# Attention and a gated block on one core: the order of work planned with a clock per engine

## The chip, the cores and the metric

The kernel runs on 1 core of one Trainium2 chip. The metric is the device time of one execution in microseconds; lower is better. TensorE (PE in the profile) multiplies matrices into PSUM, ScalarE (ACT) does the exponentials, VectorE (DVE) and GpSimd (POOL) do elementwise work, SyncE (SP) issues the DMAs.

## The reference

One transformer block over 2048 rows of 640 columns, in bf16, with 32 heads of 20 columns:

```
def _A_ref(x, wqkv, wo):                                   # H = 32, Dh = 20
    qkv = (x @ wqkv).reshape(B, S, 3, H, Dh).transpose(2, 0, 3, 1, 4)
    q, k, v = qkv[0], qkv[1], qkv[2]
    scores = einsum("bhqd,bhkd->bhqk", q, k) * (Dh ** -0.5)
    o = einsum("bhqk,bhkd->bhqd", softmax(scores), v)
    return o.transpose(0, 2, 1, 3).reshape(B, S, D) @ wo
def _B_ref(x, w_gate, w_up, w_down):                       # F = 1728
    return ((x @ w_gate) * (x @ w_up)) @ w_down

h  = x + _A_ref(layernorm(x), A_wqkv, A_wo)
h2 = h + _B_ref(layernorm(h), B_w_gate, B_w_up, B_w_down)
```

The scores are 32 x 2048 x 2048 numbers, and each goes through an exponential.

## The kernel before

Heads are taken four at a time (a group; 8 groups `g`), each head on 32 partitions. The queries are cut into four blocks of 512 (`b`, a pass; the last block also in halves `A` and `B` for six of the groups), the keys into 16 tiles of 128 (`kt`). One **unit** is the scores of one head, one key tile and 512 queries: a matmul with 32 rows of weights (`L427`) into one PSUM bank. Three units in a row fill a **score tile** `sc` of three banks, of which there are two buffers; ScalarE makes one exponential over its 1536 columns into `E` (`L433`, six buffers). The **value matmuls** (`L597`) multiply `E` with the values and a column of ones; four heads sum side by side in one PSUM bank `acc`, over all keys of a group and a block (a **segment**). VectorE copies `acc` out (`L607`, `L612`); GpSimd multiplies by the reciprocals of the sums (`L529`).

Everything else that TensorE does is a **job**, a generator that stands in a queue: transposes of the first layer norm (`job_T`, `L252`), projections to queries and keys (`job_proj`, `L270`), values (`job_V`, `L284`), and, when all groups of a query block are done, that block's tail: the output projection (`out_mm`, `L812`), the second layer norm (`ln2_pieces` on VectorE, then transposes), the two gated sums (`glu_sum`, `L878`) and the last product (`job_y`, `L911`). All jobs share one PSUM bank `mi`, which VectorE empties before the next job may fill it. The layer norm pieces of VectorE stand in a second queue, `aux`; the first layer norm's square root is made on GpSimd in small steps, and VectorE's reciprocal (`L212`) waits for them.

VectorE also makes the exponentials of 80 units itself: for 20 segments, `emit_x` makes one unit per head with a score matmul of its own into `mi` (`L453`); `L463` scales it, and five passes follow (`L474` to `L477`, and `L468`): two masks that split an int32 into exponent and mantissa, and a polynomial of the mantissa.

The program is written out in a loop over the 656 score tiles, and each engine runs its instructions in the order in which the loop emits them. Per tile: the three score matmuls and the exponential; a job begun earlier goes on for up to `BUDGET` = 640 ns; up to four 512-column value matmuls of the tiles up to two back; `aux` pieces while an estimate of VectorE's load is below `AUX_LOAD`; passes of VectorE's units; and, if no job was going on, either a new unit of VectorE's or a new job for up to `START` = 440 ns:

```
        used = go_on(BUDGET) if i < n_tiles else BUDGET
        emit_AV(i if i >= n_tiles else i - 2 if i >= LAG else i - 4)
        while now["dve"] < AUX_LOAD and step_aux():
            pass
        if not used:
            if x_todo and cur["fresh"] and now["dve"] < X_LOAD and x_ready():
                emit_x()
            else:
                begin(START)
```

The estimate `now["dve"]` grows with each instruction given to VectorE and falls by `STEP` = 1331 ns with each tile. After the last tile, `last_tail` does the last 256 rows with all of TensorE; a second path, `general`, is in the program and is skipped unless the sums leave their range.

Of the kernel before, what the change touches and what calls it, by code (L numbers as in the profile page):

```python
# [12 lines left out]
I32 = mybir.dt.int32  # L13
ACT = mybir.ActivationFunctionType
# [32 lines left out]
SUM_HI = 1e15  # L47
NEXT = "next slot"
END = "end"
BUDGET = 640  # L50
START = 440
WARM = 58
LAG = 10
STEP = 1331
AUX_LOAD, X_LOAD = 1200, 900
SHIFT = 394.0
X_AHEAD, X_STEP, X_OUT = 8, 5, 6
LOG2E = 1.4426950408889634
X_SCALE = SM_SCALE * LOG2E * 2.0 ** 23
C3 = 0.07802454279127117  # L60
X_P, X_Q, X_R = -0.10261439735317812, 6.123365857342997, 5.794771205884579
EXP_BIAS = (SHIFT * SM_SCALE * LOG2E - 127.0) / LOG2E - math.log(C3) - SHIFT * SM_SCALE


@with_exitstack
def kernel(
# [153 lines left out]
    now = {"i": 0, "dve": 0}  # L220

    def dve(ns):

        now["dve"] += ns
# [71 lines left out]
    for ch in range(NB):  # L296
        for g in range(G1):
# [9 lines left out]
    X_KT = 2  # L307
    X_SEGS = [s for s, (p, g, _, _, kind) in enumerate(segs)
              if kind == "only" and p in "012"]

    tiles, cur_t, pos = [], [], 0
    for s, (p, g, lo, hi, _) in enumerate(segs):
        w = PASS[p][2]
        n = BANK // w
        for kt, j, k in [(kt, j, k) for kt in range(lo, hi, n) for j in range(HPG) for k in range(n)]:
            if s in X_SEGS and X_KT <= kt < X_KT + n:
                continue
            cur_t.append((s, kt + k, j, pos))
            pos += w
            if pos == EW:  # L320
                tiles.append((cur_t, EW))
                cur_t, pos = [], 0
# [3 lines left out]
    first_tile = {}  # L326
    for i, (us, _) in enumerate(tiles):
        for s, *_ in us:
            first_tile.setdefault(s, i)
    x_todo = deque((first_tile[s] - X_AHEAD + X_STEP * j, s, j) for s in X_SEGS for j in range(HPG))  # L330
    x_pieces = deque()
    x_made = {}
    x_put = []
    x_live = {"units": 0, "passes": 0}
# [6 lines left out]
    urgent = deque()  # L341
    aux = deque()
# [6 lines left out]

    def do(key, fn, front=False):  # L350
        def gen():
            fn()
            yield 0
        add(key, gen(), front)
# [9 lines left out]
    def step():  # L364
        if urgent and cur["fresh"]:
            if cur["gen"] is not None:
                jobs.appendleft((cur["key"], cur["gen"]))
            cur["key"], cur["gen"] = urgent.popleft()
# [4 lines left out]
        try:  # L373
            c = next(cur["gen"])
        except StopIteration:
            done.add(cur["key"])
            cur["gen"], c = None, END
        cur["fresh"] = c in (END, NEXT)
        return c
# [6 lines left out]
    def step_aux():  # L386
        while aux:
            try:
                dve(next(aux[0]) or 200)
# [3 lines left out]
        return False  # L393

# [5 lines left out]
    def go_on(ns):  # L400
        used = 0
        while not cur["fresh"] and used < ns:
            c = step()
            used += c if c not in (END, NEXT) else 0
        if not cur["fresh"]:
            return max(used, 1)
        return used

    def begin(ns):
        used = 0  # L410
        while used < ns:
            c = step()
            if c is None or c == NEXT or (c == END and used):
                break
            used += c if c != END else 0

    def emit_S(i):
# [6 lines left out]
        for s, kt, j, o in us:  # L424
# [6 lines left out]
                start=True, stop=True)  # L431
        e = ep.tile([P, EW], BF16, name="E")
        nc.scalar.activation(e[:, 0:n], sc[:, 0:n], ACT.Exp, bias=EXP_BIAS, scale=SM_SCALE)  # L433
        for s, kt, j, o in us:
            av_q.append((i, s, kt, j, e[:, o:o + PASS[segs[s][0]][2]]))

    def x_ready():
        due, s, _ = x_todo[0]
        p, g = segs[s][0:2]
        return (due <= now["i"] and x_live["units"] < X_OUT and x_live["passes"] < 2  # L440
                and ("q", PASS[p][0], g) in done and ("k", g, 0) in done)

    def emit_x():

        _, s, j = x_todo.popleft()
        p, g = segs[s][0:2]
        b, c0, w = PASS[p]
        n = BANK // w
        ensure(("k", g, X_KT // TPB))
        ensure(("q", b, g))  # L450
        ps = bank()
        for k in range(n):
            nc.tensor.matmul(  # L453
                ps[:, k * w:(k + 1) * w],
                lhsT=kT[g][SLOT * j:SLOT * (j + 1), (X_KT + k) * P:(X_KT + k + 1) * P],
                rhs=q_of(g, b, c0, w)[SLOT * j:SLOT * (j + 1), :],
                start=True, stop=True)
        v = xp.tile([P, BANK], I32, name="xv", bufs=2)
        m = xp.tile([P, BANK], F32, name="xm")
        t = xp.tile([P, BANK], F32, name="xt")  # L460
        e = xp.tile([P, BANK], BF16, name="xe", bufs=X_OUT)
        dve(690)
        nc.vector.tensor_scalar(v[:], ps[:], X_SCALE, 0.0, ALU.mult, ALU.max)  # L463
        x_live["units"] += 1
        x_live["passes"] += 1

        def last():
            nc.vector.scalar_tensor_tensor(e[:], t[:], X_R, v[:].bitcast(F32), ALU.add, ALU.mult)  # L468
            x_live["passes"] -= 1
            x_made.setdefault(s, []).append((j, e))  # L470
            if len(x_made[s]) == HPG:
                x_put.append([(now["i"], s, X_KT + k, j, e[:, k * w:(k + 1) * w]) for k in range(n) for j, e in x_made[s]])
        x_pieces.extend([
            (430, lambda: nc.vector.tensor_scalar(m[:].bitcast(I32), v[:], 0x007FFFFF, 0x3F800000, ALU.bitwise_and, ALU.bitwise_or)),  # L474
            (430, lambda: nc.vector.tensor_scalar(v[:], v[:], 0x7F800000, None, ALU.bitwise_and)),
            (690, lambda: nc.vector.scalar_tensor_tensor(t[:], m[:], X_P, m[:], ALU.add, ALU.mult)),  # L476
            (690, lambda: nc.vector.scalar_tensor_tensor(t[:], t[:], X_Q, m[:], ALU.add, ALU.mult)),  # L477
            (690, last)])

    def put_x():  # L480

        for units in x_put:
            s = units[0][1]
            at = next((k for k, u in enumerate(av_q) if u[1] > s), len(av_q))
            for u in reversed(units):
                av_q.insert(at, u)
        x_put.clear()

    def step_x(n):
        while n > 0 and x_pieces:  # L490
            ns, fn = x_pieces.popleft()
            dve(ns)
            fn()
            n -= 1

    def need_x(s):
        while len(x_made.get(s, ())) < HPG:
            if x_pieces:
                step_x(1)
                continue  # L500
            while not cur["fresh"]:
                step()
            emit_x()
# [64 lines left out]
    def emit_AV(upto):  # L568
# [9 lines left out]
        if acc["seg"] != s:  # L578
            if now["i"] < acc["from"]:
# [3 lines left out]
        most = 2 * QB * 2 // w  # L583
# [7 lines left out]
        for _ in range(ready):  # L591
            _, _, kt, j, e = av_q.popleft()
            if s in X_SEGS and kt == X_KT:
# [8 lines left out]
        acc["left"] -= ready  # L602
        if acc["left"] == 0:
# [9 lines left out]
            acc["seg"], acc["from"] = None, now["i"] + 2  # L613
# [81 lines left out]
    def gen_ln(ch):  # L695
        ts = range(ch * TPB, (ch + 1) * TPB)
        mv = small.tile([P, TPB, 2], F32, name="mv")
        while ch not in xs:
            yield STEP
# [89 lines left out]
    def new_st(rows_of):  # L789
# [3 lines left out]
        st["hh"] = [hp.tile([P, QB], BF16, name=f"hh{f}") for f in range(2 * FP)]  # L793
# [40 lines left out]
    def job_out(on, st, ts, key):  # L834
        pairs = [ts[k:k + 2] for k in range(0, len(ts), 2)]

        def T_pair(pair):
            for t in pair:
                while ("l2", key, t) not in done and end["pool"] is None and key is not None:
                    yield NEXT  # L840
# [48 lines left out]

    def job_glu(st, ts, order=tuple(range(FP))):  # L890
        c0, n = ts[0] * P, len(ts) * P
        hold = {}
        for k, fp in enumerate(order):
# [3 lines left out]
            for f2 in range(2):  # L897
                for m in range(2):
# [32 lines left out]
    def add_tail(b, ts):  # L931
# [16 lines left out]
        do(("load",) + key, ready)  # L948
# [255 lines left out]
```

## Time and profile before

| what | us |
|---|---|
| time, median of 3 runs (lowest, highest) | 978.65 (976.43, 979.57) |
| span of the profiled execution | 977.6 |
| ScalarE busy | 905.2 (93%) |
| of this, the 656 exponentials, L433 | 887.8 |
| TensorE busy in matmuls | 865.3 (89%) |
| VectorE busy | 576.8 (59%) |
| GpSimd busy | 64.6 (7%) |
| mean granted TensorE clock | 0.935 |

The span runs from the first instruction to the last of one profiled execution; the profiled execution has no device time of its own, and the median of the timed runs lies 1.05 us above its span. A group line of the profile names line, engine, operation, output and inputs with their shapes and the count, then the busy time, the mean of one instruction in ns, and the engine's idle time just before them with what ended it. In a timeline line the first two numbers are start and length in us. In a window line the columns are length, busy time of PE, PEld, DVE, ACT and POOL with counts, the granted clock, the DMA share and GB/s.

### The profile page before, as it was taken

How to read it: one execution, taken by the hardware profiler on the slowest of the kernel's cores; microseconds unless marked ns; L12 is line 12 of the kernel's file. 1: busy time of each engine (PE TensorE's matmuls, PEld its weight loads, DVE VectorE, ACT ScalarE, POOL GpSimd, SP SyncE). 2: the span in 40 equal slices, each digit the busy share in tenths (PEclk: the TensorE clock that was granted, in tenths of full speed). 3: DMA queues.
4: the chain of work that ended last, by engine and by line, in shares of the span. 5: the costliest groups of instructions: out<-in, count | busy, mean ns of one | idle time of the engine just before them, and what ended most of it. 6: DMA issues, size and time to landing. Idle time of an engine off the chain costs nothing.

```text
span 977.6 us, 17623 instructions
## 1 busy us (share of the span) xinstructions
PE 865.3 (89%) x6981; PEld 325.1 (33%) x7041; DVE 576.8 (59%) x1186; ACT 905.2 (93%) x692; POOL 64.6 (7%) x163
## 2 busy tenths in 40 slices
PE   6779998889989899999898988898889999989987
PEld 4223332222223222233232222233332333435455
DVE  7564367877777777777677677777143331143232
ACT  6689999999999899999999999999899999999941
POOL 4110001200000000000000000000000000000000
PEclk9999999999999599999778899999597999989989
DMA  6000000010014022101420222000602000211210
GB/s 182 4 24 1 1 25 24 13 32 27 5 47 146 12 66 59 40 13 33 180 67 12 66 67 60 12 22 23 163 1 66 14 13 20 67 36 40 81 35 17
DMA packets 67816, 44.42 MB, mean 45 GB/s; under 512 B 18504, under 2 KB 63404, under 8 KB 67728
## 3 DMA queue, kind: packets, MB, share of 16 engines
q1 hardware_dynamic: 67728, 43.23, 15.5%
q8 instruction: 57, 0.93, 0.4%
q14 instruction: 31, 0.25, 0.1%
HBM read 35.91 MB, written 7.30 MB: 44 GB/s over the span
## 4 chain that ended last, share of the span: by engine, by line
ACT 44%; PE 32%; issue 13%; DVE 9%; POOL 1%; ACTq 0%; DVEq 0%; POOLq 0%
ACT E L433 44%; PE sc L427 8%; PE acc L597 6%; PE mi L878 3%; PE mi L270 3%; PE mi L812 2%; PE mi L284 2%; PE mi L911 2%; PE f L878 2%; DVE xv L463 1%; PE mi L453 1%; DVE st L176 1%; PE f L911 1%; PE mi L252 1%; DVE vx L239 1%
## 5 line engine op out<-in xcount | busy, mean ns | idle before, releaser
L433 ACT ACTIVATE E<-sc 128x1536 bf16<-128x1536 f32 x656 | 887.8, 1662 | 30.4 <-PE sc L427 29.7
L427 PE MATMUL sc<-qa,kT 32*128 32x512 bf16 x1456 | 205.9, 406 | 41.3 <-ACT E L433 35.0
L597 PE MATMUL acc<-E,vx 128*32 128x512 bf16 (+1 forms) x2352 | 215.6, 374 | 5.3 <-DVE vx L239 4.1
L427 PEld LDWEIGHTS <-kT 32*128 32x128 bf16 x2352 | 89.8, 92 | 260.8 <-issue 251.0
L597 PEld LDWEIGHTS <-vx 128*32 128x32 bf16 x2432 | 56.6, 94 | 159.7 <-issue 151.9
L270 PE MATMUL mi<-lnT,wp 128*128 128x512 bf16 x282 | 84.7, 382 | 9.7 <-DVE kT L277 2.3
L427 PE MATMUL sc<-qb,kT 32*128 32x256 bf16 (+1 forms) x896 | 72.0, 301 | 13.8 <-ACT E L433 13.0
L529 POOL TENSOR_TENSOR on<-asb,bc 128x512 bf16<-128x512 f32 (+1 forms) x30 | 34.5, 1150 | 714.7 <-DMA bc<-scr 507.1
L463 DVE TENSOR_SCALAR xv<-mi 128x512 int32<-128x512 f32 x80 | 55.0, 688 | 29.9 <-PE mi L453 26.3
L911 PE MATMUL mi<-wd,hh 128*128 128x320 bf16 x378 | 68.4, 303 | 3.6 <-DVE xv L463 3.5
L239 DVE CAST u<-mi 128x512 bf16<-128x512 f32 (+3 forms) x56 | 34.9, 624 | 56.2 <-PE mi L878 56.0
L886 DVE TENSOR_TENSOR hh<-mi,u 128x512 bf16<-128x512 f32 (+3 forms) x56 | 34.9, 624 | 55.0 <-PE mi L878 54.9
L878 PE MATMUL mi<-ln2T,wu 128*128 128x512 bf16 (+2 forms) x188 | 55.2, 385 | 4.6 <-DVE xv L463 3.0
L468 DVE SCALAR_TENSOR_TENSOR xe<-xt,xv 128x512 bf16<-128x512 f32 x80 | 56.6, 707 | 2.0
L477 DVE SCALAR_TENSOR_TENSOR xt<-xt,xm 128x512 f32<-128x512 f32 x80 | 56.3, 704 | 0.9
L476 DVE SCALAR_TENSOR_TENSOR xt<-xm 128x512 f32<-128x512 f32 x80 | 55.7, 697 | 0.0
L878 PE MATMUL mi<-ln2T,wg 128*128 128x512 bf16 (+2 forms) x187 | 52.3, 372 | 2.2 <-issue 0.8
L911 PEld LDWEIGHTS <-hh 128*128 128x128 bf16 x448 | 37.5, 97 | 40.1 <-issue 29.8
L915 DVE TENSOR_TENSOR xr<-mi,xr 128x320 bf16<-128x320 f32 x27 | 13.3, 492 | 51.3 <-PE mi L911 51.3
L812 PE MATMUL mi<-wo,on 128*128 128x320 bf16 x224 | 41.8, 311 | 0.7 <-DVE xv L463 0.4
L607 DVE COPY asb<-acc 128x512 f32<-128x512 f32 (+1 forms) x34 | 20.2, 594 | 34.5 <-PE acc L597 32.3
L277 DVE TENSOR_SCALAR kT<-mi,one_row 128x512 bf16<-128x512 f32 x31 | 23.2, 749 | 29.0 <-PE mi L270 29.0
(143 smaller groups left out, 637.0 us busy)
## 6 DMA issues: line engine op xcount, KB each, us to landing
bc<-scr SPq DMA_DIRECT2D x100, 64.0 KB
wu<-in_B_w_up_dram SPq DMA_DIRECT2D x20, 320.0 KB
wg<-in_B_w_gate_dram SPq DMA_DIRECT2D x20, 320.0 KB
qsp<-qa SPq DMA_DIRECT2D x8, 384.0 KB
xr<-in_A_x_dram SPq DMA_DIRECT2D x16, 160.0 KB
out_dram<-xr SPq DMA_DIRECT2D x14, 160.0 KB
wd<-in_B_w_down_dram SPq DMA_DIRECT2D x13, 160.0 KB
xs<-in_A_x_dram SPq DMA_DIRECT2D x3, 640.0 KB
```

The costliest lines, as they stand in the source:

```text
L239: nc.vector.tensor_copy(dst, src)
L270: nc.tensor.matmul(ps[:], lhsT=wslice(m, g, c), rhs=lnT[:, c, ch * QB:(ch + 1) * QB], start=(c == 0), stop=(c == KT - 1))
L427: nc.tensor.matmul(sc[:, o:o + w], lhsT=kT[g][SLOT * j:SLOT * (j + 1), kt * P:(kt + 1) * P], rhs=q_of(g, b, c0, w)[SLOT * j:SLOT * (j + 1) ...
L433: nc.scalar.activation(e[:, 0:n], sc[:, 0:n], ACT.Exp, bias=EXP_BIAS, scale=SM_SCALE)
L463: nc.vector.tensor_scalar(v[:], ps[:], X_SCALE, 0.0, ALU.mult, ALU.max)
L468: nc.vector.scalar_tensor_tensor(e[:], t[:], X_R, v[:].bitcast(F32), ALU.add, ALU.mult)
L476: (690, lambda: nc.vector.scalar_tensor_tensor(t[:], m[:], X_P, m[:], ALU.add, ALU.mult)),
L477: (690, lambda: nc.vector.scalar_tensor_tensor(t[:], t[:], X_Q, m[:], ALU.add, ALU.mult)),
L597: nc.tensor.matmul(acc["t"][SLOT * j:SLOT * (j + 1), 0:w], lhsT=vx[kt][:, VS * h:VS * h + SLOT], rhs=e, start=(acc["n"][j] == 0), stop=(ac ...
L812: nc.tensor.matmul(ps[:, 0:HALF], lhsT=on[g][:, t * P:(t + 1) * P], rhs=wo[g][:, cs], start=(g == 0), stop=(g == NG - 1))
L878: nc.tensor.matmul(ps[0:M, 0:n], lhsT=st["w", fp][k][:, c, f2 * P:f2 * P + M], rhs=st["ln2T"][:, c, c0:c0 + n], start=(c == 0), stop=(c == ...
L911: nc.tensor.matmul(ps[:, 0:HALF], lhsT=st["hh"][f][0:K, t * P:(t + 1) * P], rhs=late["Wd"][f][0:K, cs], start=(f == 0), stop=(f == 2 * FP ...
```

## The change

The loads and budgets per tile give way to a plan with a clock per engine. `at` holds, in ns, when TensorE, VectorE and ScalarE will be done with what they have been given, when each score buffer will be free, and when the banks `mi` and `acc` will be. Constants give the cost of a score tile, of an exponential by its columns, of a switch between kinds of matmul, and of a hand-over.

- Jobs: `run_job` begins a job only if it can do a minimal piece (`LEAST`, or the whole for transposes and values) before TensorE must make the next score tile, and then goes on until that time. There is no piece of a fixed size any more.
- Values: up to eight 512-column matmuls follow each other (16 of 256 columns), and they are emitted when eight are ready.
- VectorE's units: no score matmul of their own. For a full tile of the first three blocks, where the plan says that ScalarE does not wait for the tile and that VectorE is free, VectorE takes the third bank (`x_takes`, `emit_x`), and the exponential covers only the first two. The arithmetic is in units of bf16's bits: a scale, one mask pass, and three passes with a polynomial, the last of which writes int16 that is read as bf16.
- `aux` and the passes of VectorE's units go out where VectorE has time left until TensorE's next score tile (`spare`).
- Tails: transposes that wait for their layer norm are set aside (`WAIT`) and a last-product job may run meanwhile; the last product is two jobs per block; the first half of the last block may go ahead of the second of these; its gated sums are made in pairs in one bank (`glu_pair`).
- The range test of the sums compares their bits as integers.

```diff
-BUDGET = 640
-START = 440
-STEP = 1331
-AUX_LOAD, X_LOAD = 1200, 900
-X_AHEAD, X_STEP, X_OUT = 8, 5, 6
+EXP_NS, EXP_END, EXP_COL = 50, 166, 5 / 6
+S_NS, S_EXP, SWITCH, LAT = 323, 445, 110, 150
+TOL, LEAST = 200, 430
+X_LEAST, X_OUT = 4, 6
...
     def dve(ns):
-        now["dve"] += ns
+        ready = at["pe"] + LAT
+        spare(ready)
+        at["dve"] = max(at["dve"], ready) + ns
...
-            if s in X_SEGS and X_KT <= kt < X_KT + n:
-                continue
...
+    def spare(until):
+        while at["dve"] + (x_pieces[0][0] if x_pieces and not aux else 600) <= until + TOL:
+            if not step_aux() and not step_x():
+                break
...
+    COST = {"T": 300, "v": 680}
+    def run_job(until):
+        if cur["fresh"]:
+            key = urgent[0][0] if urgent else cur["key"] if cur["gen"] is not None else jobs[0][0] if jobs else None
+            if key is None or max(at["pe"], at["mi"]) + SWITCH + COST.get(key[0], LEAST) > until:
+                return
+        while at["pe"] + 216 <= until + 60:
+            if step() in (None, NEXT, END):
                 break
...
+        begin = max(at["pe"], at["slot"][-2])
+        at["pe"] = begin + S_NS
+        start = max(at["exp"], begin + S_EXP)
+        n_act, took = n, None
+        if start == at["exp"] and x_takes(i):
+            n_act = n - BANK
+            took = emit_x(sc[:, n_act:n], [(s, kt, j, o - n_act) for s, kt, j, o in us if o >= n_act])
         e = ep.tile([P, EW], BF16, name="E")
-        nc.scalar.activation(e[:, 0:n], sc[:, 0:n], ACT.Exp, bias=EXP_BIAS, scale=SM_SCALE)
+        exps = nc.scalar.activation(e[:, 0:n_act], sc[:, 0:n_act], ACT.Exp, bias=EXP_BIAS, scale=SM_SCALE)
...
+        run = EXP_NS + n_act * EXP_COL
+        free = start + run + EXP_END
+        at["slot"].append(free if took is None else max(free, at["dve"] + LAT))
+        at["exp"] = start + run
...
+    def x_takes(i):
+        us, n = tiles[i]
+        s = us[-1][0]
+        return (n == EW and segs[s][4] == "only" and (PASS[segs[s][0]][0] < LAST_B or not jobs and not cur["gen"]) and last_tile[s] - i >= X_LEAST and len({u[0] for u in us}) == 1
+                and len(x_pieces) < 3 and at["dve"] < at["pe"] + TOL and x_live["units"] < X_OUT)
...
-            (430, lambda: nc.vector.tensor_scalar(m[:].bitcast(I32), v[:], 0x007FFFFF, 0x3F800000, ALU.bitwise_and, ALU.bitwise_or)),
-            (430, lambda: nc.vector.tensor_scalar(v[:], v[:], 0x7F800000, None, ALU.bitwise_and)),
-            (690, lambda: nc.vector.scalar_tensor_tensor(t[:], m[:], X_P, m[:], ALU.add, ALU.mult)),
-            (690, lambda: nc.vector.scalar_tensor_tensor(t[:], t[:], X_Q, m[:], ALU.add, ALU.mult)),
-            (690, last)])
+            (480, lambda: nc.vector.tensor_scalar(m[:], v[:].bitcast(I32), 0x7FFF, 0x8000, ALU.bitwise_and, ALU.bitwise_or)),
+            (700, lambda: nc.vector.scalar_tensor_tensor(t[:], m[:], X_A, m[:], ALU.mult, ALU.mult)),
+            (700, lambda: nc.vector.scalar_tensor_tensor(t[:], t[:], X_B, m[:], ALU.add, ALU.mult)),
+            (700, last)])
...
-        most = 2 * QB * 2 // w
+        most = 2 * HPG * QB // w
...
+        at["pe"] += SWITCH + -(-ready // HPG) * w * 5 // 12
...
-                    yield NEXT
+                    yield WAIT
...
-        used = go_on(BUDGET) if i < n_tiles else BUDGET
...
-        if not used:
-            if x_todo and cur["fresh"] and now["dve"] < X_LOAD and x_ready():
-                emit_x()
-            else:
-                begin(START)
+        if i < n_tiles:
+            run_job(max(at["exp"] - S_EXP, at["slot"][-2]))
+            spare(max(at["pe"], at["slot"][-2]))
```

## The prediction

> **What bounds the kernel now.** I read the page first, its busy row, its clock row and its chain, then the timeline of ScalarE alone, then windows around the places where ScalarE waits.
>
> ```profile
> PE 865.3 (89%) x6981; PEld 325.1 (33%) x7041; DVE 576.8 (59%) x1186; ACT 905.2 (93%) x692; POOL 64.6 (7%) x163
> PEclk9999999999999599999778899999597999989989
> ACT 44%; PE 32%; issue 13%; DVE 9%; POOL 1%; ACTq 0%; DVEq 0%; POOLq 0%
> L433 ACT ACTIVATE E<-sc 128x1536 bf16<-128x1536 f32 x656 | 887.8, 1662 | 30.4 <-PE sc L427 29.7
> ```
>
> ScalarE is busy for 93% of the span, nearly all of it in 656 exponentials; its idle time before them is ended by the score matmuls. So the time is the exponentials' own rate plus the places where TensorE brings a score tile late. The timeline of ScalarE shows both (start, length, count, idle time before):
>
> ```profile
> 16.07 9.51 ACT L433 ACTIVATE E<-sc 128x1536 bf16<-128x1536 f32 x7 [0.66 <-PE sc L427]
> 30.24 1.45 ACT L433 ACTIVATE E<-sc 128x1536 bf16<-128x1536 f32 x1 [4.66 <-PE sc L427]
> ...
> 37.55 2.79 ACT L433 ACTIVATE E<-sc 128x1536 bf16<-128x1536 f32 x2 [2.39 <-PE sc L427]
> ...
> 73.69 1.45 ACT L433 ACTIVATE E<-sc 128x1536 bf16<-128x1536 f32 x1 [2.59 <-PE sc L427]
> ...
> 332.14 1.45 ACT L433 ACTIVATE E<-sc 128x1536 bf16<-128x1536 f32 x1 [0.97 <-PE sc L427]
> ...
> 707.47 35.03 ACT L433 ACTIVATE E<-sc 128x1536 bf16<-128x1536 f32 x26 [0.72 <-PE sc L427]
> ...
> 933.62 1.28 ACT L1082 ACT_TABLE_LOAD   x1
> ```
>
> Unhindered, 26 exponentials take 35.03 us; less the last one's 1.662 that is 33.37 over 25, or **1.335 us each**. The first starts at 16.07 and the table load behind the last at 933.62, so the phase is 917.5 us. 656 x 1.335 is 875.8; **41.7 us are lateness**. Adding up run by run (a run's start, less the one before, less 1.335 per exponential) gives 14.3 us up to 77.06; 15.8 us where the granted clock is low (mostly 295 to 342, 499 to 571 and 700 to 745); 11.6 us scattered. The windows and single rows tell what the low clock is:
>
> ```profile
> 345.00:478.00 133.00, 120.68 (x870) 40.92 (x878) 101.66 (x175) 133.00 (x101) 7.33 (x5) 1.00 0.17 50
> 478.00:504.00 26.00, 23.40 (x142) 6.20 (x142) 15.91 (x27) 25.18 (x20) 1.49 (x1) 0.61 0.52 176
> ```
> ```profile
> 478.10 0.39 PE L427 MATMUL sc<-qa,kT 32*128 32x512 bf16 x3 [0.95 <-ACT E L433]
> 478.43 0.57 PE L597 MATMUL acc<-E,vx 128*32 128x512 bf16 x4
> ...
> 482.13 0.61 PE L427 MATMUL sc<-qa,kT 32*128 32x512 bf16 x3 [0.19 <-ACT E L433]
> 482.68 0.62 PE L597 MATMUL acc<-E,vx 128*32 128x512 bf16 x4
> ```
>
> The seventh column of a window is the granted clock. With jobs on TensorE it is 1.00, and ScalarE is busy for all of the 133 us. At 475 the jobs of a block end, only scores and values remain, and at 478.5 the matmuls slow by half; the loss comes only when jobs return at the slow clock, and 3 to 6 us later the clock is back.
>
> **The change, part by part.**
>
> *Exponentials.* In the order of the changed program 683 score tiles hold all 2048 units of 512 columns. 95 tiles leave their third bank to VectorE (94 between tile 86 and 512, one at 619) and the last tile is short: 587 exponentials of 1536 columns and 96 of 1024. The trace has no 1024. The slope between the 128x512 activation at L691 (0.687) and a lone 1536 (1.45) is 0.745 ns a column, 0.38 us for 512; a third of 1.335 is 0.445; the casts at L236 (256 columns 0.377, 640 columns 0.692) give 0.82 ns, 0.42 us. I take 0.42, the same engine's slope between two measured sizes, so 0.915 us. Then 587 x 1.335 = 783.6, 96 x 0.915 = 87.8, together 871.4: **-4.4 us** (-0.6 to -6.8).
>
> *The start.* VectorE runs in order. At 22.04 GpSimd begins the chain of small steps to the root (done 27.08, 5.0 us); VectorE's reciprocal stands behind one copy of values only, so the next copies, TensorE's value jobs and score tile 7 wait: 4.66 idle. In the changed order the reciprocal stands behind two such copies, next to a projection needed only by tile 10. Walking on with the rows (scores 0.45, projection 1.24, its copy 0.75), tile 10 still waits for both projections of its group, but is 4.0 late where the old one is 8.2. The second reciprocal stands behind four copies instead of directly behind the transposes' copies; the 2.59 at 73.69 goes. The value jobs around 53 to 61 (idle 0.64, 0.26, 0.38, 0.31) are placed only where they fit. Together -7.0 (0 to -10): 14.3 becomes 7.3.
>
> *Uncut jobs and values by eight.* There are 510 groups of value matmuls before, 262 after, and 80 score matmuls into the job bank go. Each group begins with 0.1 to 0.23 us without a weight load in the rows, so TensorE gets back 30 to 60 us. None of that is on the path where ScalarE is unhindered; it is what lets scattered lateness (value jobs at 131 to 156, output jobs, 11.6 in all) shrink. One of these was VectorE's mask pass at 191.17, 3.75 us instead of 0.468, while GpSimd's eight memsets ran for 4.64 us; there is one such pass per unit now instead of two, on 95 units instead of 80, so it may recur (0 to 2.2). New are score tiles that are due 0.42 us sooner and their bank's second reader. I put the 11.6 at 6.0 (2.5 to 15.6): **-5.6**.
>
> *The low clock.* The changed order has four long stretches with no job (14, 54, 38 and 6 tiles) and four waits of 5 to 7 tiles before the second layer norm's transposes; before there were two of about 15 and four of 5 or 6. The clock will fall in each. During a stretch nothing is lost: at the low clock scores take 0.55 and eight values 1.0, so 2.67 tiles cost 2.5 us against 3.2 us of ScalarE with a third of the tiles short. When jobs return, pieces are up to five 512-column matmuls (0.43 each slow, 2.3 us) instead of three, but every second or third tile has no job and catches up. About 2 us at each of eight places: 16, against 15.8 now. **0** (-10 to +20).
>
> *VectorE.* A unit costs 0.688+0.468+0.439+0.697+0.704+0.707 = 3.70 us now (group rows L463, L474 to L477, L468) and loses the 0.439 pass: 3.26. With int32 in and int16 out, which no row shows, the nearest rows bound a pass between 0.468 and 0.751 (L277); I take the three-operand rows. 95 x 3.26 less 80 x 3.70 is +14 us, 590 of 960 busy. Hidden: the first pass starts about a microsecond before ScalarE reaches the tile. In the stretches where every third tile gives a unit, 3.26 stands against 3.58; without that cover each unit delays a score tile by the excess.
>
> *The rest.* The paired gate sums, the split output jobs, the set-aside transposes and the bit test of the sums lie behind ScalarE or at the end with rows of the same size; the order shows that no output job is left to fill a wait: 0. Behind the last score tile 16 value matmuls stand instead of 24: -0.3. The 44.0 us after the exponentials stay.
>
> **Sum.** 16.07 + 871.4 + (7.3 + 6.0 + 15.8) + 44.0 - 0.3 = 960.3 of span against 977.6. The median of the runs lies 1.05 above the profiled span; 961.3, so 961 us.
>
> **Rivals.** (1) The clock stays up through the stretches and its lateness goes: -16, 945 us. [...] Against it: here the clock fell at 478.5 with no gap on TensorE above 0.95 us. (2) The lateness only moves: the start keeps its waits on GpSimd and VectorE's two readers cost what the scattered 5.6 gave; only the exponentials' 4.4 and little else remain, about 975. (3) Slower: uncut jobs at the low clock. Scores 0.55, eight values 1.0 and a piece of 2.3 are 3.85 us against 1.335 and a lead of some 0.6, 1.9 late; three such intervals before the clock returns, nine places, is 51 instead of 16: +35, 996 us. It decides from 34 us on (16 plus the 17.3 gained), 3.8 us a place. For it: 253 tiles have no job behind them against 56. Against it: the empty tiles between pieces.
>
> **How the numbers follow.** The forecast, with its bounds about 950 to 973, gets 0.65; rival 1 0.12; rival 2 0.11, half of it within 0.3% (2.9 us, about what a measurement of this kernel can tell from no change); rival 3, with VectorE late as a smaller part, 0.12. Faster is 0.65+0.12+0.05 = 0.82, same 0.06, slower 0.12. Leaving out most of rival 3 and the better half of rival 1, the range is 944 to 984.
>
> **What would show it.** Right: short exponentials about 0.42 shorter; idle time before 80 us halved; clock low in the four long stretches with ScalarE unhindered there; idle of some 2 us at each return of jobs. Wrong: idle of 4 us or more at each return; score tiles released by VectorE rather than ScalarE; an exponential of 1024 columns near 1.3; clock 1.00 through the empty stretches.

## The result and the profile after

The changed kernel takes 994.96 us (median of 4 runs, 993.0 to 995.55) where the kernel before takes 979.11 us beside it: ratio 1.0158, 95% interval 1.0136 to 1.0181. It is slower by 1.6%; 961 us had been forecast. The profiled span is 993.9 us against 977.6, and the mean granted clock of TensorE 0.898 against 0.935.

The page of the changed kernel: busy times, the granted clock in 40 slices, the chain of waits by engine, and the group of the exponentials.

```profile
PE 854.9 (86%) x7041; PEld 326.5 (33%) x7041; DVE 588.3 (59%) x1181; ACT 912.0 (92%) x719; POOL 66.2 (7%) x163
PEclk9999999999687999965587999965789999789998
PE 43%; ACT 33%; issue 14%; DVE 8%; DMA 1%; POOL 0%; ACTq 0%; SPq 0%; DVEq 0%; POOLq 0%
L456 ACT ACTIVATE E<-sc 128x1536 bf16<-128x1536 f32 (+1 forms) x683 | 894.5, 1405 | 41.6 <-PE sc L443 34.4
```

Three things differ. The clock row stands at 7 or below in ten slices instead of five. ScalarE, 44% of the chain before, is 33% now and TensorE 43%: the path runs more through TensorE. And ScalarE's idle time before exponentials is 41.6 us, up from 30.4; score matmuls end 34.4 of it, 29.7 before.

ScalarE's groups kept apart by shape show the shortened exponentials at work:

```profile
L456 ACT ACTIVATE E<-sc 128x1536 bf16<-128x1536 f32 x587 | 811.3, 1466 | 39.5 <-PE sc L443 33.3 <-PE acc L610 2.6
L456 ACT ACTIVATE E<-sc 128x1024 bf16<-128x1024 f32 x96 | 99.2, 1033 | 2.2 <-PE sc L443 1.2
```

And the timeline of ScalarE (start, length, count, idle before) shows the start, and the table load that ends the phase:

```profile
15.98 10.90 ACT L456 ACTIVATE E<-sc 128x1536 bf16<-128x1536 f32 x8 [0.66 <-PE sc L443]
28.60 2.79 ACT L456 ACTIVATE E<-sc 128x1536 bf16<-128x1536 f32 x2 [1.73 <-PE acc L610]
32.91 21.63 ACT L456 ACTIVATE E<-sc 128x1536 bf16<-128x1536 f32 x16 [1.51 <-PE sc L443]
55.74 42.18 ACT L456 ACTIVATE E<-sc 128x1536 bf16<-128x1536 f32 x31 [1.21 <-PE sc L443]
...
951.44 1.28 ACT L1129 ACT_TABLE_LOAD   x1
```

The idles of 4.66, 2.39 and 2.59 us are gone; 1.73, 1.51 and 1.21 stand in their place. The loss came later.

**A ledger of lateness.** To place it, I cut every profile by one rule. An interval goes from the start of one exponential to the start of the next; unhindered it is 1.331 us, after a short exponential 0.905 us (the shortest short one is 0.904). The excess is lateness. It is put to the start (the first 40 score tiles), else to the low clock (the interval touches a stretch of granted clock 0.5, or the 4 us after one), else to the rest.

| kernel | span | back to back | start | low clock | rest | last exponential to end | time at low clock |
|---|---|---|---|---|---|---|---|
| before | 977.6 | 871.8 | 14.6 | 19.9 | 9.8 | 45.5 | 109 |
| after | 993.9 | 867.3 | 5.4 | 32.8 | 28.9 | 43.5 | 198 |
| difference | +16.3 | -4.5 | -9.2 | +12.9 | +19.1 | -2.0 | +89 |

(Each row is one profiled execution. The cut is a little different from the prediction's, which gave 14.3, 15.8 and 11.6 for before.) Two items pay for the loss: the low clock, and many small lags at full clock, 67 intervals over 0.15 us late, 20.4 us together, where before there were 19 with 7.4.

**Inside a stretch without jobs.** ScalarE's timeline at the low clock, tiles 303 to 356:

```profile
452.67 3.71 ACT L456 ACTIVATE E<-sc 128x1536 bf16<-128x1536 f32 x3 [0.34 <-PE sc L443]
456.82 3.71 ACT L456 ACTIVATE E<-sc 128x1536 bf16<-128x1536 f32 x3 [0.45 <-PE sc L443]
460.98 9.61 ACT L456 ACTIVATE E<-sc 128x1536 bf16<-128x1536 f32 x8 [0.44 <-PE sc L443]
...
501.55 1.45 ACT L456 ACTIVATE E<-sc 128x1536 bf16<-128x1536 f32 x1 [1.62 <-PE sc L443]
```

Three exponentials, one of them short, then 0.45 us of waiting for scores: just what the short one had saved. The 54 tiles of this stretch hold 15 short exponentials, which save 6.4 us, and are 5.8 us late; the 38 tiles from 475 on hold 11, save 4.7 and are 4.6 late. Then, at 501.55, the return of jobs costs its 1.62 us.

**Among jobs, at full clock.** All engines around score tiles 233 to 237:

```profile
335.71 0.69 DVE L899 TENSOR_TENSOR hh<-mi,u 128x512 bf16<-128x512 f32 x1 [0.37 <-PE mi L891]
335.92 0.10 PEld L891 LDWEIGHTS <-wu 128*128 128x128 bf16 x1 [0.23 <-issue]
...
336.45 1.02 PE L891 MATMUL mi<-ln2T,wu 128*128 128x512 bf16 x4 [0.46 <-DVE hh L899]
...
337.41 0.10 PEld L443 LDWEIGHTS <-kT 32*128 32x128 bf16 x3 [0.42 <-issue]
337.41 0.39 PE L443 MATMUL sc<-qa,kT 32*128 32x512 bf16 x3
...
337.73 0.61 PE L610 MATMUL acc<-E,vx 128*32 128x512 bf16 x5
337.96 0.38 PE L610 MATMUL acc<-xe,vx 128*32 128x512 bf16 x1
337.97 0.59 PE L610 MATMUL acc<-E,vx 128*32 128x512 bf16 x2
338.49 0.10 PEld L891 LDWEIGHTS <-wu 128*128 128x128 bf16 x1 [0.42 <-issue]
338.49 0.39 PE L891 MATMUL mi<-ln2T,wu 128*128 128x512 bf16 x1
...
338.81 0.39 PE L443 MATMUL sc<-qa,kT 32*128 32x512 bf16 x3
338.92 0.69 DVE L247 CAST u<-mi 128x512 bf16<-128x512 f32 x1 [1.20 <-PE mi L891]
...
339.66 0.81 PE L891 MATMUL mi<-ln2T,wg 128*128 128x512 bf16 x3 [0.46 <-DVE u L247]
```

TensorE loads a new job's weights at 335.92, but its first matmul must wait 0.46 us until VectorE has emptied the bank; the same at 339.66. The 0.42 us of issue at 337.41 and 338.49 are idle time of the weight loads alone; matmuls run beside it (the job's four until 337.47). From matmul to matmul a change of kind costs about 0.10 us: at full clock 0.312 us at the median from a job's 512-column matmul to the scores, or from values to a job, against 0.216 within a job. The plan charges 0.11 us for a fresh job, which fits, but nothing for going on with a cut one, and it takes VectorE's copy as ready before the job's last matmul is counted. It also counts eight values as two rounds of four heads side by side. The eight from 337.73 on take three rounds: a unit of VectorE's (`xe`) stands out of the heads' turn, and the last matmul starts only at 338.18. So tiles with work on TensorE are longer than planned.

I set TensorE's time from score tile to score tile (from weight load to weight load) against the plan's own clock, for the 74 intervals at full clock after which ScalarE was over 0.15 us late: together they are 20.2 us longer than planned, about the size of what the rest gained. Eight values and three projection matmuls, the commonest, take 2.17 us at the median (6 cases), planned 1.62; eight values and the scores alone 1.08 (4 cases, each with a third round), planned 0.86. From matmul to matmul the 74 are 16.4 us longer than planned: 5.8 us are waits of a job's first matmul (13.7 against 7.9 planned), 5.4 us rounds of values (16.2 against 10.8); the remainder was not separated. The 74 were picked because ScalarE was late behind them, so these sums show the size, and the runs below must show the cause. And `run_job` fills up to the time at which the next score tile is due, with nothing kept back.

### The profile page after: what moved, and what is told of

The parts are those of the page before. It is cut to its first block, busy times and chain, and to the rows that moved or that the text cites. A ratio compares the mean times of both kernels' runs of the same rounds, so it can differ in the third digit from the quotient of the medians.

```text
span 993.9 us, 17723 instructions
## 1 busy us (share of the span) xinstructions
PE 854.9 (86%) x7041; PEld 326.5 (33%) x7041; DVE 588.3 (59%) x1181; ACT 912.0 (92%) x719; POOL 66.2 (7%) x163
## 3 DMA queue, kind: packets, MB, share of 16 engines
q1 hardware_dynamic: 67728, 43.23, 15.5%
## 4 chain that ended last, share of the span: by engine, by line
PE 43%; ACT 33%; issue 14%; DVE 8%; DMA 1%; POOL 0%; ACTq 0%; SPq 0%; DVEq 0%; POOLq 0%
ACT E L456 33%; PE sc L443 11%; PE acc L610 10%; PE mi L891 6%; PE mi L946 5%; PE mi L278 4%; PE f L891 2%; PE mi L825 1%; PE mi L292 1%; PE mi L909 1%; PE f L946 1%; DVE qa L285 1%; DVE kT L285 1%; DVE vx L247 1%; DVE hh L899 1%
## 5 line engine op out<-in xcount | busy, mean ns | idle before, releaser
L456 ACT ACTIVATE E<-sc 128x1536 bf16<-128x1536 f32 (+1 forms) x683 | 894.5, 1405 | 41.6 <-PE sc L443 34.4
L481 DVE TENSOR_SCALAR xv<-sc 128x512 f32<-128x512 f32 x95 | 65.5, 690 | 64.9 <-PE sc L443 63.6
L443 PE MATMUL sc<-qb,kT 32*128 32x256 bf16 (+1 forms) x896 | 72.6, 307 | 16.9 <-ACT E L456 15.9
L486 DVE SCALAR_TENSOR_TENSOR xe<-xt,xv 128x512 int16<-128x512 f32 x95 | 68.5, 721 | 1.2
L492 DVE SCALAR_TENSOR_TENSOR xt<-xm 128x512 f32<-128x512 int32 x95 | 66.5, 700 | 2.0
L247 DVE CAST u<-mi 128x512 bf16<-128x512 f32 (+1 forms) x42 | 29.0, 690 | 41.5 <-PE mi L891 41.2
L946 PEld LDWEIGHTS <-hh 128*128 128x128 bf16 x448 | 39.6, 98 | 39.7 <-issue 26.5
L891 PE MATMUL mi<-ln2T,wu 128*128 128x512 bf16 (+1 forms) x170 | 47.9, 396 | 3.9 <-DVE hh L899 3.9
L891 PE MATMUL mi<-ln2T,wg 128*128 128x512 bf16 (+1 forms) x170 | 45.7, 381 | 5.3 <-DVE u L247 5.2
L899 DVE TENSOR_TENSOR hh<-mi,u 128x512 bf16<-128x512 f32 (+1 forms) x42 | 28.9, 687 | 33.3 <-PE mi L891 33.1
L278 PEld LDWEIGHTS <-wp 128*128 128x128 bf16 x310 | 26.5, 97 | 57.6 <-issue 40.8
L491 DVE TENSOR_SCALAR xm<-xv 128x512 int32<-128x512 int32 x95 | 45.0, 474 | 0.6
```

The lines of the kernel that those rows point to most:

```text
L278: nc.tensor.matmul(ps[:], lhsT=wslice(m, g, c), rhs=lnT[:, c, ch * QB:(ch + 1) * QB], start=(c == 0), stop=(c == KT - 1))
L443: nc.tensor.matmul(sc[:, o:o + w], lhsT=kT[g][SLOT * j:SLOT * (j + 1), kt * P:(kt + 1) * P], rhs=q_of(g, b, c0, w)[SLOT * j:SLOT * (j + 1) ...
L456: exps = nc.scalar.activation(e[:, 0:n_act], sc[:, 0:n_act], ACT.Exp, bias=EXP_BIAS, scale=SM_SCALE)
L481: took = nc.vector.tensor_scalar(v[:], ps, X_SCALE, X_BASE, ALU.mult, ALU.max)
L486: nc.vector.scalar_tensor_tensor(e[:], t[:], X_C, v[:], ALU.add, ALU.add)
L491: (480, lambda: nc.vector.tensor_scalar(m[:], v[:].bitcast(I32), 0x7FFF, 0x8000, ALU.bitwise_and, ALU.bitwise_or)),
```

## The experiments

The theories: (1) the plan prices job pieces and hand-overs too low and packs to the deadline; (2) eight value matmuls in a row hold up the next scores; (3) shorter exponentials and the score tile's second reader, VectorE, make tiles late; (4) the low clock, which the long stretches without jobs bring. Each was timed beside the kernel before; the ledger's columns are from one profiled execution of each.

| kernel | time, us | ratio to before (interval) | back to back | start | low clock | rest | time at low clock |
|---|---|---|---|---|---|---|---|
| after | 994.96 | 1.0158 (1.0136–1.0181) | 867.3 | 5.4 | 32.8 | 28.9 | 198 |
| e1_reserve | 987.05 | 1.0090 (1.0057–1.0123) | 866.8 | 12.4 | 28.3 | 16.8 | 147 |
| e2_four | 996.51 | 1.0182 (1.0138–1.0226) | 868.1 | 10.8 | 28.0 | 29.1 | 181 |
| e3_nounits | 1014.22 | 1.0358 (1.0320–1.0396) | 907.7 | 7.9 | 20.2 | 20.1 | 290 |
| e4_busy | 978.10 | 0.9999 (0.9981–1.0016) | 867.3 | 5.4 | 17.1 | 29.2 | 44 |
| e5_before_eight | 981.64 | 1.0044 (1.0020–1.0067) | 871.8 | 16.5 | 23.0 | 9.2 | 116 |
| e6_costs | 991.76 | 1.0154 (1.0114–1.0193) | 866.8 | 25.5 | 18.4 | 20.3 | 82 |
| e7_costs_busy | 994.13 | 1.0168 (1.0132–1.0203) | 866.8 | 25.5 | 17.5 | 21.8 | 58 |
| e8_before_busy | 973.84 | 0.9957 (0.9928–0.9986) | 871.8 | 16.4 | 18.8 | 6.9 | 75 |
| e9_costs_110 | 978.68 | 1.0002 (0.9973–1.0031) | 866.0 | 5.5 | 26.5 | 17.8 | 106 |
| e10_costs_110_busy | 970.26 | 0.9922 (0.9894–0.9951) | 866.0 | 8.0 | 17.2 | 20.2 | 44 |
| e11_reserve40_busy | 968.13 | 0.9899 (0.9866–0.9932) | 867.3 | 5.5 | 12.1 | 17.9 | 55 |
| e12_long_in_stretch | 996.11 | 1.0187 (1.0165–1.0209) | 877.9 | 5.4 | 25.1 | 29.9 | 218 |

The rest is a sum over the intervals that remain behind the start and at full clock: 514 before, 461 after, 408 in e3_nounits, 586 in e4_busy.

**e1_reserve**: job pieces end 300 ns earlier.

```diff
-            run_job(max(at["exp"] - S_EXP, at["slot"][-2]))
+            run_job(max(at["exp"] - S_EXP, at["slot"][-2]) - 300)
```

> The changed kernel, but a job may use TensorE only until 300 ns before the time at which the plan wants the next score tile; everything else the same. The changed kernel takes 994.96 us; its exponentials end 67 us later than their own rate allows, about 39 of it at the full clock and behind the start. Theory 1 (the plan prices a job's pieces and the hand-over of the job bank too low and packs to the deadline, so each error makes a score tile late): 20 to 30 us go, 965 to 975 us. Theory 2 (eight value matmuls in a row stand in front of score tiles), theory 3 (the shorter exponentials and the second reader of the third bank want the score tiles too soon) and theory 4 (the low clock): nothing that they blame changes, 990 to 1000 us.

The rest falls by 12.1 us, as theory 1 says, but 7.0 us of that go back at the start, where projections to keys now come late (2.51 us at tile 20, 4.38 at tile 25). The time lands between the two forecasts.

**e2_four**: values by four unless twelve wait (222 groups of four, 138 of eight, against 250 of eight).

```diff
-        most = 2 * HPG * QB // w
+        most = (2 if len(av_q) >= 12 * QB // w else 1) * HPG * QB // w
```

> The changed kernel with value matmuls by four, and by eight only where twelve units or more are queued: 222 groups of four and 138 of eight instead of 250 of eight. Theory 2: half of the long groups are gone, and about half of the lateness at the full clock, 975 to 985 us. Theory 1: 110 more groups, each with 0.1 to 0.3 us of switching on TensorE, in a plan that has no reserve: 995 to 1005 us. Theories 3 and 4: 990 to 1000 us.

The rest stays (29.1), and so does the time. Theory 2 falls.

**e3_nounits**: VectorE takes no third bank, so it makes no exponentials and all but the last short tile are long.

```diff
-        return (n == EW and ...
+        return (False and n == EW and ...
```

> The changed kernel without VectorE's units: ScalarE takes all three banks of every tile. The exponentials get longer by 95 x 0.426 = 40.5 us, 1035 us if nothing else changes. Theory 3: 25 us or more of the lateness goes with the short tiles and the second reader, 1003 to 1012 us. Theory 1: the plan still packs to the deadline at wrong prices, but has fewer tiles with little room and an idle VectorE: 1020 to 1032 us. Theories 2 and 4: 1030 to 1038 us.

The exponentials back to back are 40.4 us longer and lateness 18.9 us less. The rest keeps 20.1 us with no short tile and no second reader, so theory 3 explains 8.8 us of it at most (4.7 us over the 401 intervals that count as rest in both kernels). Values by eight never take a third round here; in the changed kernel they do in 67 of 155 tiles at full clock. The time, 1014.22, lies between the forecasts of theories 3 and 1. More telling is the low clock: it lasts 290 us here, half as long again as after, yet costs 20.2 us, no more than before: with long exponentials only, a slow TensorE costs less.

**e4_busy**: 220 extra 128x128x512 matmuls whose result nobody reads, where the plan shows TensorE free and no job can go on.

```diff
+            had = at["pe"]
             run_job(max(at["exp"] - S_EXP, at["slot"][-2]))
+            if i >= LAG and at["pe"] == had and cur["fresh"] and cur["gen"] is None and (waiting or not jobs and not urgent):
+                k = int((at["slot"][-2] - max(at["pe"], at["mi"]) - 2 * SWITCH) // 216)
+                if k > 0:
+                    ps = bank()
+                    for _ in range(k):
+                        nc.tensor.matmul(ps[:], lhsT=ident[:], rhs=kT[0][:, 0:BANK], start=True, stop=True)
```

> The changed kernel with 220 extra matmuls of 128x128 by 512, whose results nobody reads, in the places where TensorE has no job at all or only waiting ones, as many as the plan's idle time before the next score tile holds. They are to keep the clock up. Theory 4: the lateness at the low clock (22 us) and that at the returns of jobs go, 965 to 975 us, granted clock 0.95 or more. Theories 1 to 3: at most the 22 us go, and the 45 at the full clock stay, 975 to 990 us.

The same 75 us in windows, the changed kernel first, then e4_busy (length, busy PE, PEld, DVE, ACT, POOL with counts, granted clock, DMA share, GB/s):

```profile
425.00:500.00 75.00, 56.56 (x348) 12.34 (x346) 55.06 (x91) 70.92 (x58) 4.35 (x3) 0.59 0.26 88
```
```profile
425.00:500.00 75.00, 66.48 (x464) 20.96 (x457) 56.38 (x95) 73.72 (x61) 4.36 (x3) 0.93 0.26 88
```

116 more matmuls in the window, and the clock goes from 0.59 to 0.93; ScalarE does three more exponentials in the same time. Its timeline has one unhindered run where the stretch was broken every three exponentials:

```profile
434.42 3.71 ACT L456 ACTIVATE E<-sc 128x1536 bf16<-128x1536 f32 x3 [0.45 <-PE sc L443]
438.57 58.22 ACT L456 ACTIVATE E<-sc 128x1536 bf16<-128x1536 f32 x47 [0.44 <-PE sc L443]
```

The low clock's lateness falls from 32.8 to 17.1, and the kernel is 17 us faster, level with the one before. The rest (29.2) is untouched, and 978.10 lies where theories 1 to 3 put it, above theory 4's 965 to 975. Theory 4 holds for its part, and only for that.

**e5_before_eight**: the kernel before, with values by eight.

```diff
-        most = 2 * QB * 2 // w
+        most = 2 * QB * 4 // w
```

> The kernel before with one thing of the change: value matmuls wait until eight are ready (252 groups of eight instead of 510 of four), everything else as before. Theory 1 (the new plan packs job pieces up to the deadline at prices that are too low) and theory 4 (low clock) put nothing on the groups: 973 to 982 us, exponentials' lateness outside the start and the low clock 8 to 13 us (9.8 before). Theory 2 (eight in a row hold up the next scores) gives 984 to 992 us and that lateness 16 to 25 us.

The rest stays at 9.2: theory 2 falls here too. The kernel is 0.4% slower, by the ledger in the start and the low clock; this was not followed further.

**e6_costs**: dearer prices for job work up to tile 500: 300 ns to enter a job or to go on with one that was cut, and VectorE's copy ready 216 ns later (`cur["to"]` is 300, and `cur["last"]` 216 while a job is being written out).

```diff
-        ready = at["pe"] + LAT
+        ready = at["pe"] + LAT + cur["last"]
...
-            at["pe"] = max(at["pe"], at["mi"]) + SWITCH
+            at["pe"] = max(at["pe"], at["mi"]) + cur["to"]
+        elif cur["cut"] and c not in (END, NEXT):
+            at["pe"] += cur["to"]
...
-        while at["pe"] + 216 <= until + 60:
+        while at["pe"] + 216 + (cur["to"] if cur["cut"] else 0) <= until + 60:
```

> The changed kernel with the plan's prices for job work set nearer to what the trace shows, up to tile 500: entering or resuming a job 300 ns instead of 110 or nothing, and an eviction ready only after the job's last matmul. No reserve is kept. Theory 1: lateness outside the start and the low clock falls from 28.9 us to 12 to 18 us, the start stays at 5 to 9 us, time 974 to 984 us. If the prices are not the cause, that lateness stays at 25 to 30 us and the time at 990 to 997 us.

A miss: 991.76. ScalarE's timeline shows where:

```profile
59.97 6.82 ACT L464 ACTIVATE E<-sc 128x1536 bf16<-128x1536 f32 x5 [5.86 <-PE sc L451]
75.91 4.26 ACT L464 ACTIVATE E<-sc 128x1536 bf16<-128x1536 f32 x3 [9.12 <-PE sc L451]
```

Fewer jobs fit per tile, so keys that a score tile needs are not made in time, and the tile waits while they are (`ensure`): 5.86 and 9.12 us here, and 4.18 of lateness at tile 105. TensorE's timeline before the second:

```profile
70.00 1.49 PE L293 MATMUL mi<-wv,lnT 128*128 128x320 bf16 x5 [0.58 <-DVE vx L248]
72.07 2.29 PE L279 MATMUL mi<-lnT,wp 128*128 128x512 bf16 x5 [0.58 <-DVE vx L248]
74.30 0.61 PE L451 MATMUL sc<-qa,kT 32*128 32x512 bf16 x2
75.21 0.61 PE L451 MATMUL sc<-qa,kT 32*128 32x512 bf16 x4 [0.31 <-DVE kT L286]
```

Job follows job with no score tile between them, and the tile's own third matmul still waits for VectorE's copy of the keys. The start costs 25.5 us. From 75 us on, all lateness is 38.9 us against 61.7 after. At the start the plan's low prices serve better: there the due time of the jobs decides, not the next score tile.

**e7_costs_busy**: e6_costs with the insertion of e4_busy, which finds room for only 39 matmuls.

> The same prices, and 39 unread 128x128x512 matmuls in tiles where TensorE has no job. Theories 1 and 4 together: the low clock's lateness falls to 15 to 22 us beside the 12 to 18 us outside it, time 964 to 976 us, under the kernel before. Were the two gains the same microseconds, no better than the better of the two alone: 974 to 984 us.

A miss for the same reason; the start is as bad (25.5), and the 39 matmuls bring nothing that can be seen.

**e8_before_busy**: the kernel before, with two such matmuls in each of 31 empty tiles.

```diff
                 begin(START)
+                if i >= LAG and i < n_tiles and cur["fresh"] and cur["gen"] is None and not jobs:
+                    ps = bank()
+                    for _ in range(2):
+                        nc.tensor.matmul(ps[:], lhsT=ident[:], rhs=kT[0][:, 0:BANK], start=True, stop=True)
```

> The kernel before with 62 unread 128x128x512 matmuls, two in each of 31 tiles with no job and no unit. Theory 4: the low clock goes from 109 us to under 60 us, its lateness from 19.9 to 8 to 14 us, time 966 to 973 us. If the low clock costs the kernel before nothing (its score tiles are 1.331 us long and leave room), 975 to 980 us.

0.4% faster, between the two forecasts. The low clock lasts 75 us instead of 109, where under 60 had been expected, and its lateness hardly moves (18.8 against 19.9, not 8 to 14), so the gain is not shown to come from there. The clock costs the kernel before little that these matmuls could save.

**e9_costs_110**: e6_costs with its dearer prices only for tiles 110 to 539.

> The same dearer prices for job work (300 ns to enter or resume a job, evictions ready after the last matmul) only for tiles 110 to 539, where no key is due soon. Theory 1: the start stays at 5.4 us, lateness outside the start and the low clock falls from 28.9 us to 14 to 20 us, time 976 to 984 us. If e6 lost its time to dearer prices themselves and not to keys that came late (tiles 9 to 25 and 105), it stays at 988 to 995 us.

The start stays at 5.5 and the rest falls from 28.9 to 17.8: 978.68, within the forecast. Nothing but the prices was changed, and 16 us came back: 11.1 off the rest, as theory 1 says, and 6.3 off the low clock, which lasts 106 us instead of 198. The 300 ns are more than the 0.10 us of a change of kind, so they also act as a reserve; how much is price and how much reserve, the runs do not separate.

**e10_costs_110_busy**: e9_costs_110 with the insertion of e4_busy, 76 matmuls.

> The kernel of e9_costs_110 with 76 unread 128x128x512 matmuls where TensorE has no job. Theories 1 and 4 together: both terms fall, 17 to 22 us at the low clock and 14 to 20 us outside it, time 960 to 971 us, under the kernel before. Were the two gains the same microseconds: 976 to 984 us.

970.26, 0.8% under the kernel before. The low clock costs 17.2 instead of 26.5. The gains add only in part: the changed kernel's time falls by 16.9 us with the matmuls alone (e4_busy), by 16.3 with the prices alone, and by 24.7 with both, since the prices had already taken 6.3 us off the low clock. Two causes there are: e4_busy leaves the rest as it was, and the prices lower it.

**e11_reserve40_busy**: e4_busy with e1_reserve's 300 ns from tile 40 on, 116 matmuls.

```diff
-            run_job(max(at["exp"] - S_EXP, at["slot"][-2]))
+            run_job(max(at["exp"] - S_EXP, at["slot"][-2]) - (300 if i >= 40 else 0))
```

> The kernel of e4_busy with e1_reserve's 300 ns kept back from the jobs only from tile 40 on, and 116 unread matmuls. Theories 1 and 4 together: start 5.4 us, low clock 17 to 22 us, outside 14 to 19 us, time 961 to 970 us. If the reserve did not take effect by the hand-over, outside 25 to 30 us and 974 to 980 us, as in e4_busy.

968.13, the fastest of all, 1.0% under the kernel before (0.9899, 0.9866 to 0.9932) and, by the two ratios, about 2.5% under the changed one. Its page:

```profile
PEclk9999999999989899999699999999999999889899
ACT 44%; PE 31%; issue 17%; DVE 7%; POOL 0%; ACTq 0%; DVEq 0%; POOLq 0%
L456 ACT ACTIVATE E<-sc 128x1536 bf16<-128x1536 f32 (+1 forms) x683 | 885.2, 1462 | 19.2 <-PE sc L443 14.6
```

ScalarE's share of the chain is back at 44%, and its idle time before exponentials is 19.2 us instead of 41.6. In its timeline one run of 78 stands where the changed kernel's run from 55.74 ended after 31:

```profile
55.62 103.50 ACT L456 ACTIVATE E<-sc 128x1536 bf16<-128x1536 f32 x78 [1.21 <-PE sc L443]
```

**e12_long_in_stretch**: no third bank for VectorE at tiles 303 to 356 and 475 to 512, so 71 short exponentials instead of 96.

```diff
+        if 303 <= i < 357 or 475 <= i < 513:
+            return False
```

> The changed kernel with no third bank taken by VectorE in the two long stretches of tiles without a job (303 to 356 and 475 to 512): 25 of the 96 short exponentials become long again, so the exponentials back to back are 25 x 0.426 = 10.7 us longer. If a short exponential in such a stretch brings nothing at the low clock (theory 4: TensorE cannot deliver a score tile and eight values in 0.905 us there), lateness falls by about as much: time 990 to 998 us, low-clock lateness 21 to 26 us instead of 32.8. If the stretches' lateness has another cause, lateness stays and the time is 1001 to 1008 us.

25 short exponentials fewer make the exponentials 10.6 us longer back to back, and the time only about 1 us (996.11; the spans differ by 3.4). ScalarE's timeline over the first of the two stretches:

```profile
425.17 76.13 ACT L456 ACTIVATE E<-sc 128x1024 bf16<-128x1024 f32 x57 [0.27 <-PE sc L443]
502.77 6.91 ACT L456 ACTIVATE E<-sc 128x1536 bf16<-128x1536 f32 x5 [1.47 <-PE sc L443]
```

57 exponentials in one run, all long but the first (whose shape the line shows) and the last, though the granted clock from 425 to 500 us is 0.55. The two stretches are 0.6 and 0.3 us late instead of 5.8 and 4.6. So VectorE's units bring almost nothing there while the clock is low; in e4_busy, with the clock up, the same two stretches keep their 26 short exponentials and are 2.0 and 0.3 us late.

## Why the prediction was wrong, point by point

- **Exponentials, -4.4**: right. The counts are as forecast, the short one starts its successor 0.426 us sooner (forecast 0.42), and back to back they take 4.5 us less.
- **The start, -7.0**: right, and somewhat better: -9.2.
- **VectorE, +14 us, hidden**: right in its own time, 588.3 us busy against the 590 forecast, and as a second reader: TensorE's waits before scores are ended by exponentials (75.9 us), and none by VectorE's read of the third bank. Its units still cost TensorE the third rounds of values, which the prediction did not have.
- **The rest, -0.3**: -2.0 in the ledger, one execution against another.
- **The low clock, 0**: a failed step, +12.9. It had two halves. "About 2 us at each of eight places" where jobs return was right: outside the stretches ten intervals over 0.9 us late, at seven places, sum to 15.5. (In the kernel before the clock was back 1.9, 5.8 and 6.5 us after the jobs' returns at 497.15, 701.44 and 738.28, where the prediction has 3 to 6.) "During a stretch nothing is lost" was wrong: 12.5 of the 32.8 us lie inside the stretches (the remaining 4.8 are small). The working set 2.5 us of TensorE against 3.2 of ScalarE over 2.67 tiles, an average. But the scores and the eight values do not come evenly: at the low clock they take 0.55 + 1.0 = 1.55 us together where the values go in two rounds (0.98 us to the next matmul, 10 groups; 1.39 in three rounds, 30 groups), and behind a short exponential ScalarE is back after 0.905. Two score buffers do not bridge that, so each short exponential is paid back with some 0.44 us. e12_long_in_stretch and e4_busy show it from both sides.
- **Scattered lateness, -5.6, bounds 2.5 to 15.6**: the larger failure. The rest is 28.9 us, far beyond that; +19.1 in place of -5.6, 24.7 us of the 33.6 by which the forecast span (960.3) was missed. The step took TensorE's saving from fewer groups of values (30 to 60 us) as slack that shortens the lags. (It read 0.1 to 0.23 us a group off idle weight loads; from matmul to matmul it is 0.10.) The planner spends that slack: it gives every free nanosecond before a score tile's due time to jobs, at prices under the trace's. The prediction weighed what the instructions cost and not what the planner takes them to cost: the 0.11 in `SWITCH` fits the trace, but the plan counts the waits for the shared bank too short (7.9 us for 13.7) and the third rounds of values (0.22 us each) not at all, and keeps nothing back for either. With dearer prices (e9) or a reserve (e11) it is 17.8 or 17.9.
- **The rivals**: rival 3 gave the right time, 996, by a mechanism that the runs show only in part. Its price, 5.7 us a place, did not come: the seven returns cost 1.0 to 3.8 us, and pieces cut shorter by a reserve left the low clock's lateness at 28.3 (e1). Rival 1's world, a clock that stays up, is near what e4_busy makes by force: 15.7 us of lateness go, as its -16 said, but from a level that the rest had raised.

**Open.** 17.8 us of lateness outside the start and the low clock remain with dearer prices, 8 us over the kernel before. Short tiles carry 2.4 to 4.5 of it in the three kernels with a mended plan; where the others come from was not separated.

## What to carry to other kernels

A planner that fills each gap to its deadline turns every error of its prices into lateness of the bounding engine: compare its prices with the trace, waits for a shared bank included, and keep a reserve, except where a due time presses. Work that is gathered into long uncut blocks leaves long stretches without it, and here the clock fell in them (198 us instead of 109); a saving on the bounding engine counts only if the engine that feeds it keeps up tile by tile, not on average (25 short exponentials made long again, 10.6 us, cost about 1 us of time in e12_long_in_stretch).

## What the hardware showed unexpectedly

TensorE's clock fell here without any long idle time. The timeline of TensorE in the changed kernel, as the jobs run out:

```profile
429.12 0.39 PE L443 MATMUL sc<-qa,kT 32*128 32x512 bf16 x3 [0.93 <-ACT E L456]
430.46 0.39 PE L443 MATMUL sc<-qa,kT 32*128 32x512 bf16 x3 [0.95 <-ACT E L456]
430.79 0.62 PE L610 MATMUL acc<-E,vx 128*32 128x512 bf16 x8
431.81 0.39 PE L443 MATMUL sc<-qa,kT 32*128 32x512 bf16 x3 [0.40 <-ACT E L456]
432.73 0.61 PE L443 MATMUL sc<-qa,kT 32*128 32x512 bf16 x3 [0.53 <-ACT E L456]
```

No gap is over 0.95 us, and at 432.73 three score matmuls take 0.61 us instead of 0.39. The windows up to there and behind show the granted clock, 1.00 and then 0.50:

```profile
340.00:432.00 92.00, 83.23 (x639) 29.12 (x637) 66.73 (x111) 90.52 (x72) 4.29 (x3) 1.00 0.15 43
432.00:463.00 31.00, 24.71 (x142) 5.04 (x139) 23.09 (x39) 28.98 (x24) 1.27 (x1) 0.50 0.38 137
```

Whether the gaps or the small matmuls of the stretch brought it down, no run here separates.

What had not been expected is how little kept it up: 220 unread matmuls of some 0.22 us, 47 us of work in 978, cut the time at the low clock from 198 to 44 us and brought 17 us. And in the changed kernel at full clock (medians, 512 columns) the next weight load comes 0.42 us after the last one where values give way to scores or to a job, or a job to scores, and 0.23 us where scores give way to either, while the matmul behind a job's last starts only 0.10 us later than within a job (0.312 against 0.216).
